# Half of a weight quarter in units 7 and 9 as separate transfers of eight partitions

## The chip, the core and the metric

The kernel runs on one core of a Trainium2 chip. The core has five engines with a queue of instructions each: TensorE (PE), VectorE (DVE), ScalarE (ACT), GpSimd (POOL) and SyncE (SP). They synchronise by semaphores. Data between the main memory and the on-chip memory of 128 partitions is moved by sixteen DMA engines, which all queues share. To tell the two kinds apart, this text always says "DMA engine" for one of those sixteen. The metric is the device time of one execution in microseconds: the median over several executions. The time before is 437.35 us, the median of three runs (436.70 to 437.56).

## The reference

The reference joins two parts. The first is causal attention over eight batches, eight heads, 576 tokens and a head size of 64, with a decay bias from a cumulated gate:

```
scores = scale * q @ k.T;   bias = -(cum[:, None] - cum[None, :])
attn   = softmax(where(causal, -1e9, scores + min(bias, 0)))
x      = attn @ v                      # heads side by side: 8 x 576 x 512
```

The second mixes the tokens in the frequency domain. It keeps 64 modes of the real Fourier transform over the tokens, and multiplies each mode by a complex 512 x 512 matrix of its own:

```
X  = rfft(x, axis=1)[:, :64]
Yr = Xr @ w_r - Xi @ w_i;   Yi = Xr @ w_i + Xi @ w_r      # per mode
u  = x + irfft(Y, n=576)
out = u + relu(u @ w_ch)
```

The weights w_r and w_i have 64 x 512 x 512 float32 values each, 134 MB together. They are most of the 163 MB that an execution reads.

## The kernel before

**Attention.** A loop over `n` in `range(N)` with N = 32 handles one batch and two heads at a time: transposes of q and k, scores, exponentials, and products with v. After each step the Fourier transform of the step's tokens is taken (`fft`, `fft_pick`). Every eight steps one group `g` of 128 of the 512 input channels is complete, and the mode products of that group can run.

**Weights.** The weights of the first three channel groups come in 24 *units* (`NUN`). A unit holds 16 modes of one group, either w_r (even units) or w_i (odd units). `unit_loads(u)` makes four lists for it, one for each quarter `h`: a quarter fills 32 partitions, from `QP * h` on, with 4 rows of 2048 values (`HU`) in each. Float32 in main memory becomes bf16 on the chip; the transfer itself converts. A quarter is one transfer of 512 KB as written, 1 MB as read, except where a first row is left out or a unit lies in two places. The weights of the fourth group come in 16 *tiles* of 64-partition transfers (`tile_loads`). Five buffers, `w_sb`, hold units and tiles in turn. Unit 7 lies in `w_sb0`, unit 9 in `w_sb2`.

**The list.** `loads_w(upto)` is what hands out the quarters in order: it takes list entries one by one, up to the number that `on_chip[n]` allows at step `n`. Entry `4 * u + h` is quarter `h` of unit `u`. `load(*lists)` merges the lists of one step (q and k, v, tails of v, weights) by their relative position, and issues them on POOL's queue, at line 315 of the kernel before. All loads of weights, q, k and v go through this one queue in this order, and an instruction that waits there holds up all behind it.

**Semaphores.** POOL's transfers use eight semaphores in turn. A transfer that takes a semaphore waits until the transfer before it on that semaphore has landed, so that at most eight are under way at a time. One transfer raises its semaphore sixteen times, once for each DMA engine, and only then has it landed.

**Consumers.** `quads` (line 605) multiplies a unit: unit 7 in step n = 14, unit 9 in step n = 17. `modes` (line 628) multiplies the tiles of the fourth group after the attention loop. The last tile's product is followed by the last transposes, the products with w_ch, and the sums and stores of the output, which have no more loads to wait for. SP's queue carries the small loads `qt<-ncum_dram`, two rows each, once per step from n = 2 on, and the stores.

Of the kernel before, what the change touches and what calls it, by code (L numbers as in the profile page):

```python
# [19 lines left out]
def kernel(  # L20
# [14 lines left out]
    DM = H * D  # L35
# [190 lines left out]
    HU = WM * DM  # L226

    def slot(i, x, n=1):

        return w_sb[i][:, x * WM : (x + n) * WM, :].rearrange("p m e -> p (m e)")  # L230
# [8 lines left out]
    def parts_of(u):  # L239

        if u == 0:
            return [(0, xg[:, : 4 * HU])]
        if u == 1:
            return [(0, ya[:, HU:]), (3, xg[:, 4 * HU : 5 * HU])]
        return [(0, slot(UNIT_AT[u], 0, 4))]

    wt = {}

    def unit_loads(u):

        g, c, ri = u // NCK, u % NCK // 2, u % 2
        src = (moe_w_r, moe_w_i)[ri][:, g * P : (g + 1) * P, :]
        slots, todo = [], []
        for j0, t in parts_of(u):
            slots += [t[:, i : i + HU].rearrange("p (q e) -> p q e", q=QD) for i in range(0, t.shape[1], HU)]
        for h in range(QD):
            todo.append([])
            for j0, t in parts_of(u):
                first = 1 if ri == 1 and c + h + j0 == 0 else 0
                j1 = j0 + t.shape[1] // HU  # L260
                todo[-1].append((
                    t[QP * h : QP * h + QP, first * HU :].rearrange("p (j x) -> p j x", x=HU),
                    src[16 * c + 4 * (j0 + first) + h : 16 * c + 4 * j1 - 3 + h : 4].rearrange(
                        "j (p q) e -> p j (q e)", q=QD
                    ),
                ))
        wt[g, c, ri] = slots
        return todo

    def tile_loads(k):  # L270

        c, ri = divmod(k, 2)
        src = (moe_w_r, moe_w_i)[ri][:, (NG - 1) * P :, :]
        i, x = TILE_AT[k]
        t = slot(i, 2 * x, 2).rearrange("p (m e) -> p m e", e=DM)
        m0 = 2 * MC * (c // 2) + 2 * (c % 2)
        todo = []
        for x0, x1 in [(0, 4)] if k < NT3 - 1 else [(0, 2), (2, 4)]:
            for h in range(2):
                first = 1 if ri == 1 and c == 0 and x0 + h == 0 else 0  # L280
                todo.append((
                    t[HP * h : HP * h + HP, 2 * (x0 + first) : 2 * x1].rearrange("p (m q) e -> p m (q e)", q=2),
                    src[m0 + 4 * (x0 + first) + h : m0 + 4 * x1 - 3 + h : 4].rearrange(
                        "m (p q) e -> p m (q e)", q=2
                    ),
                ))
        wt[NG - 1, c, ri] = [t[:, :WM], t[:, WM:]]
        n = len(todo) // 2
        return [todo[:n], todo[n:]]

    NLW = 4 * NUN + 2 * NT3
    asked, queued = [0], []

    def loads_w(upto):
        todo = []
        while asked[0] < min(upto, NLW):
            if not queued:
                t = asked[0]
                queued.extend(unit_loads(t // 4) if t < 4 * NUN else tile_loads((t - 4 * NUN) // 2))
            todo += queued.pop(0)  # L300
            asked[0] += 1
        return todo

# [45 lines left out]
    first = loads_qk(0)  # L349
    load(first[:2])  # L350
    load(loads_w(2 * W0), loads_v(0) + loads_tails(0) + first[2:] + loads_v(1))
    nc.sync.dma_start(out=Ff_sb.rearrange("p T c -> p (T c)"), in_=d_Ff)
    nc.sync.dma_start(out=G_sb[:, :S], in_=d_G)
# [265 lines left out]
    def modes(g, c, meanwhile=None):  # L619
# [16 lines left out]
        for x in range(4):  # L636
# [3 lines left out]
            for z in range(4):  # L640
                if meanwhile:
                    product(ri, z // 2, 2 * y + z % 2)
                else:
                    product(ri, y, z)
        load(loads_w(fits(NLW, 2 * NUN + 2 * c + 2)))
        yb = fpool.tile([P, DM], FP16, name="y_sb", tag="y")
        for cols in halves if c == NCK - 1 else [slice(0, DM)]:
# [65 lines left out]
    with tc.tile_pool(name="sc_psum", bufs=2, space=PSUM) as scpool, \  # L713
# [8 lines left out]
        for n in range(N):  # L722
            tails_due = loads_tails(n // B + 1)[n % B - 3 : n % B - 2] if 2 < n % B < 5 else []
            load((loads_qk(n + LA) if n % 2 else []) + (loads_vs(n) if n else loads_v(LA)) + tails_due, loads_w(on_chip[n]))
            if n == N - B:
                nc.gpsimd.dma_start(out=wch_sb, in_=moe_w_ch.rearrange("(dt p) e -> p dt e", p=P))
# [18 lines left out]
            i = first_pairs[n - N + len(first_pairs)] if n >= N - len(first_pairs) else None  # L745
# [346 lines left out]
    for step in (  # L1092
# [8 lines left out]
        i = int(step[1:].rstrip("ab"))  # L1101
# [34 lines left out]
```

## Time and profile before

| what | value |
|---|---|
| median of three runs | 437.35 us |
| the profiled execution's own time | 437.12 us |
| its span | 435.3 us |
| PE busy | 379.7 us (87%) |
| DVE, ACT, POOL busy | 254.8, 246.7, 136.5 us |
| POOL's DMA queue: packets' time as a share of 16 DMA engines' span | 99.2% |
| moved, mean rate | 93.14 MB as written, 214 GB/s |
| read from main memory | 163.29 MB |
| last weights have landed, PE starts on them | 400.41 us |

The span reaches from the first to the last instruction. Times in this text count from its start. The profiled execution lies 0.23 us below the median, and 1.8 us of its time lie outside of its span. Besides the views of engines, the trace holds a record of each DMA packet (start, duration, size, queue) and of each semaphore increment by a transfer. They don't name the DMA engine. But the sixteen increments of one transfer, put in order, show how far the sixteen DMA engines lie apart at that transfer.

### The profile page before, as it was taken

The numbers are of one execution on the slowest core, as the hardware profiler recorded it, in microseconds if no ns is written. First come the engines' busy times: TensorE is split into PE (matmuls) and PEld (weight loads), VectorE is DVE, ScalarE is ACT, GpSimd is POOL, SyncE is SP. The second block draws the span as 40 slices with busy tenths as digits, with TensorE's granted clock in tenths as the row PEclk, the third lists the DMA queues.
The fourth block names the chain that finished last, engine by engine and source line by source line (L and its number), as shares of the span: only waits on it lengthen the run. The fifth ranks groups of instructions, "written<-read, shape, count | busy, mean of one in ns | idle before, by whom it ended". The sixth has DMA issues, their size and how long they took to land. (4 is left out here: it accounts for less than half of the span.)

```text
span 435.3 us, 12579 instructions
## 1 busy us (share of the span) xinstructions
PE 379.7 (87%) x5371; PEld 219.1 (50%) x5371; DVE 254.8 (59%) x571; ACT 246.7 (57%) x552; POOL 136.5 (31%) x218
## 2 busy tenths in 40 slices
PE   1599999989999999999997888969885798796994
PEld 1256666645656655656654445535542355342441
DVE  7555666537766765677565466634644255461795
ACT  1377777726866855757774546536541255340894
POOL 6464242131432222323322222222222221310582
PEclk9999999999999999999999899999989799999998
DMA  9999999999999999999999999999999999994798
GB/s 165 209 209 209 212 209 208 213 214 212 211 209 212 209 209 213 211 212 206 213 210 213 211 212 212 212 214 213 213 210 212 211 211 211 208 219 96 224 374 307
DMA packets 47393, 93.14 MB, mean 214 GB/s; under 512 B 8254, under 2 KB 18234, under 8 KB 47338
## 3 DMA queue, kind: packets, MB, share of 16 engines
q0 software_dynamic: 40400, 81.28, 99.2%
q1 hardware_dynamic: 6938, 11.06, 7.5%
q8 instruction: 42, 0.69, 0.6%
q14 instruction: 13, 0.11, 0.1%
HBM read 163.29 MB, written 9.51 MB: 397 GB/s over the span
## 5 line engine op out<-in xcount | busy, mean ns | idle before, releaser
L513 ACT ACTIVATE p_sb<-sc_ps,cumt_sb 128x320 f16<-128x320 f32 (+1 forms) x384 | 160.6, 519 | 33.7 <-PE sc_ps L504 33.7
L504 PE MATMUL sc_ps<-qt,kt 128*64 128x256 bf16 (+3 forms) x640 | 95.6, 295 | 2.3 <-ACT kt L458 1.7
L504 PEld LDWEIGHTS <-kt 128*128 128x128 bf16 (+1 forms) x640 | 50.5, 126 | 62.9 <-issue 35.9
L315 POOL DMA_DIRECT2D w_sb<-in_moe_w_i_dram x62 | 35.2, 568 | 96.5 <-DMA w_sb<-in_moe_w_r_dram 33.9
L458 DVE COPY qt<-tr_ps 64x576 bf16<-64x576 bf16 x64 | 47.7, 746 | 20.2 <-PE tr_ps L454 19.9
L550 DVE RECIPROCAL rcp<-av_ps 128x5 f32<-128x5 f32 x64 | 12.4, 194 | 76.1 <-PE av_ps L545 75.9
L315 POOL DMA_DIRECT2D w_sb<-in_moe_w_r_dram x60 | 34.1, 570 | 71.4 <-DMA w_sb<-in_moe_w_r_dram 26.0
L493 PE MATMUL sc_ps<-negm,ident 128*128 128x512 bf16 x128 | 51.4, 401 | 0.0
L475 ACT ACTIVATE p<-sc_ps,cumt 128x64 f16<-128x64 f32 x32 | 10.0, 314 | 58.3 <-PE sc_ps L471 58.3
L545 PEld LDWEIGHTS <-p_sb 128*128 128x128 f16 x1088 | 40.4, 98 | 3.5
L454 PE MATMUL tr_ps<-ident,qk 64*64 64x64 bf16 x1152 | 31.6, 198 | 11.8 <-DVE kt L458 5.2
L454 PEld LDWEIGHTS <-qk 64*64 64x64 bf16 x1152 | 24.3, 112 | 24.1 <-DVE kt L458 8.3
L458 ACT COPY kt<-tr_ps 64x576 bf16<-64x576 bf16 x32 | 22.9, 717 | 23.5 <-DVE qt L458 23.0
L496 PE MATMUL sc_ps<-negm,ident 128*128 128x256 bf16 x128 | 36.1, 282 | 0.0
L545 PE MATMUL av_ps<-va,p_sb 128*128 128x65 f16 x768 | 34.7, 193 | 0.0
L605 PE MATMUL yp<-w_sb,xs 64*32 64x512 bf16 (+1 forms) x704 | 30.5, 403 | 4.4 <-DMA w_sb<-in_moe_w_i_dram 1.6
L551 DVE TENSOR_TENSOR x_all<-av_ps,rcp 128x320 f16<-128x320 f32 x64 | 31.5, 492 | 2.2
L617 DVE TENSOR_TENSOR y_acc<-yp,y_acc 128x512 f32<-128x512 f32 x34 | 21.9, 686 | 16.2 <-PE yp L605 16.2
L545 PE MATMUL av_ps<-vb,p_sb 128*128 128x65 f16 x320 | 25.8, 194 | 0.0
L458 DVE COPY kt<-tr_ps 64x576 bf16<-64x576 bf16 x32 | 24.4, 764 | 0.4
L315 POOL DMA_DIRECT2D vr<-in_v_dram x22 | 15.2, 692 | 28.6 <-DMA w_sb<-in_moe_w_r_dram 8.2
L605 PEld LDWEIGHTS <-xs 64*32 64x32 bf16 (+1 forms) x768 | 16.3, 139 | 14.8 <-issue 7.8
(128 smaller groups left out, 530.0 us busy)
## 6 DMA issues: line engine op xcount, KB each, us to landing
w_sb<-in_moe_w_r_dram POOLq DMA_DIRECT2D x60, 512.0 KB, 17.0
w_sb<-in_moe_w_i_dram POOLq DMA_DIRECT2D x55, 512.0 KB, 16.6
out_dram<-w_sb SPq DMA_DIRECT2D x16, 512.0 KB
qk<-in_q_dram POOLq DMA_DIRECT2D x15, 288.0 KB, 12.7
qk<-in_k_dram POOLq DMA_DIRECT2D x15, 288.0 KB, 15.3
vr<-in_v_dram POOLq DMA_DIRECT2D x14, 256.0 KB, 15.5
x_all<-in_moe_w_r_dram POOLq DMA_DIRECT2D x4, 512.0 KB, 9.7
y_acc<-in_moe_w_i_dram POOLq DMA_DIRECT2D x3, 384.0 KB, 8.0
```

The lines of the kernel that those rows point to most:

```text
L315: nc.gpsimd.dma_start(out=dst, in_=src)
L454: nc.tensor.transpose(ps[rows, r, :], src[rows, r, :], ident16[rows, rows])
L458: copy(out=to[:, :, :, half * RH : half * RH + RH], in_=ps[HP * i : HP * i + HP].rearrange("d r (h p) -> d h p r", h=2),)
L493: nc.tensor.matmul(ps[:, : 2 * W], ident16, both, start=True, stop=False, skip_group_check=True)
L496: nc.tensor.matmul(ps[:, S : S + W], ident16, negm[:, NMB + m0 : NMB + m0 + W], start=True, stop=False, skip_group_check=True,)
L504: nc.tensor.matmul(ps[rows, c0 : c0 + i1 - i0], keys, qh[:, i0:i1], start=False, stop=True, skip_group_check=True,)
L513: nc.scalar.activation(out=pt[:, o : o + n_], in_=ps[:, c0 : c0 + n_], func=ACTF.Exp, bias=cumt_sb[:, x, pidx : pidx + 1], scale=0.125,)
L545: nc.tensor.matmul(ps[:, I, :NCH], lhsT, rhs, start=(i == 0), stop=(i == len(todo) - 1), skip_group_check=True,)
L550: nc.vector.reciprocal(out=rcp, in_=ps[:, :, D])
L551: nc.vector.tensor_tensor(out=x_all[:, g, b, :, D * h : D * h + D], in0=ps[:, :, :D], in1=rcp.unsqueeze(2).to_broadcast([P, NT, D]), op=AL ...
L605: nc.tensor.matmul(ps[hp][32 * j : 32 * j + 32, :], cols[k0:k1, q_, c0 : c0 + 4 * B, 4 * c + j], wt[g, c, ri][j][k0:k1, q_, :], start=(ri ...
L617: nc.vector.tensor_tensor(out=y, in0=ps[hp], in1=y, op=ALU.add)
```

## The change

In units 7 and 9 the second quarter (`h = 1`, 32 partitions) is no longer one transfer. Its first sixteen partitions are one transfer at the same place in the list. Its other sixteen are cut into four pieces, each of eight partitions: partitions 16 to 23 whole (4 rows of 2048 values, "large"); 512 values of the last row of partitions 24 to 31 ("small"); their first three rows ("large"); and the other 1536 values of their last row ("small"). The pieces go into a list of their own, `pieces`, and `loads_w` adds one of them after each odd list entry.

```
+    ONE_HALF = (7, 9)
+    pieces = []
     wt = {}

     def unit_loads(u):
...
         wt[g, c, ri] = slots
+        if u in ONE_HALF:
+            (dst, src), = todo[1]
+            todo[1] = []
+            for i, (p0, p1, j0, j1, x0, x1) in enumerate((
+                (0, 16, 0, 4, 0, HU), (16, 24, 0, 4, 0, HU), (24, 32, 3, 4, 0, DM), (24, 32, 0, 3, 0, HU),
+                (24, 32, 3, 4, DM, HU),
+            )):
+                (pieces if i else todo[1]).append((dst[p0:p1, j0:j1, x0:x1], src[p0:p1, j0:j1, x0:x1]))
         return todo
...
             todo += queued.pop(0)
+            if asked[0] % 2:
+                todo += pieces[:1]
+                del pieces[:1]
             asked[0] += 1
```

For unit 7 the entries are 28 to 31. So the first large piece comes behind entry 29, the first small one behind 31, the second large one behind 33 and the last small one behind 35, among the quarters of unit 8. For unit 9 they stand behind entries 37, 39, 41 and 43, the last two among the quarters of unit 10. Per unit POOL issues four transfers more; the bytes are the same.

The order on POOL's queue changes in a second way, since `load` merges by relative position and the weights' lists are longer: the first quarter of unit 8 now stands ahead of the q load of its step, not behind it, and so does the third quarter of unit 9. PE's instructions keep their order; the product of each of the two units waits for the semaphores of more transfers.

## Prediction

> **What bounds the kernel now.** I read the page's DMA queues first, then PE's timeline near the end, then POOL's waits, then the packet records.
>
> ```profile
> DMA packets 47393, 93.14 MB, mean 214 GB/s; under 512 B 8254, under 2 KB 18234, under 8 KB 47338
> q0 software_dynamic: 40400, 81.28, 99.2%
> q8 instruction: 42, 0.69, 0.6%
> ```
>
> POOL's queue fills the sixteen DMA engines for the whole span by this count. PE's fetches of instructions (q8, 42 packets of 16 KB) seem nothing: 0.6%. But each such packet sits on one DMA engine for 0.95 us.
>
> ```profile
> 389.00 0.67 PE L628 MATMUL yp<-w_sb,xs 128*32 128x512 bf16 x8 [0.69 <-DMA w_sb<-in_moe_w_i_dram]
> 394.73 0.68 PE L628 MATMUL yp<-w_sb,xs 128*32 128x512 bf16 x8 [0.75 <-DMA w_sb<-in_moe_w_r_dram]
> 396.89 0.65 PE L628 MATMUL yp<-w_sb,xs 128*32 128x512 bf16 x4 [0.50 <-DMA w_sb<-in_moe_w_i_dram]
> 400.41 0.65 PE L628 MATMUL yp<-w_sb,xs 128*32 128x512 bf16 x4 [1.47 <-DMA w_sb<-in_moe_w_i_dram]
> ```
>
> PE's timeline: every product near the end waits for its weights, the last until 400.41. The 34.9 us from there to 435.3 hold no load. So the time is the landing of the last weights plus a constant.
>
> ```profile
> POOL w_sb L315 <- DMA w_sb<-in_moe_w_r_dram: 59.9, 33, 3.5
> POOL w_sb L315 <- DMA w_sb<-in_moe_w_i_dram: 32.9, 20, 2.0
> POOL qk L315 <- PE tr_ps L454: 29.9, 7, 7.5
> ```
>
> POOL's waits are mostly for transfers (eight in flight), some for a buffer that PE frees.
>
> A transfer lands when the slowest of the sixteen DMA engines has done its share. All get equal shares of every transfer now, so they should keep step. The increments show that they don't. Against the first of the sixteen, the lags are, in us:
>
> ```
> at  46 us: 0 to 1.9, evenly spread
> at 127 us: 0 .31 .44 .61 .62 .68 1.20 1.45 | 1.82 1.92 2.06 2.21 2.29 2.49 2.76 3.08
> at 379 us: 0 .45 .61 .76 .93 1.76 2.20 3.72 | 4.99 5.40 5.44 5.76 6.36 6.55 6.62 6.89
> last one : 0 .07 .17 .56 .82 .83 1.75 2.74  | 4.44 4.49 4.79 5.18 5.37 5.56 5.90 6.89
> ```
>
> Eight are late and eight early, with a gap of 1.3 us between the groups at 379 us. Each 16 KB fetch in the stretch from 290 to 330 us pushes one of the late eight on by about 0.9 us, none of the early; eight times five fetches make the distance (42 x 0.95 / 8 = 5.0 us). So the last landing, 400.37, is a late one's; the last early one is done at 393.48 + 2.74 = 396.22.
>
> **The change part by part.** *Shares.* A packet of 2048 values (8 KB read, 4 KB written) takes 0.322 us and the next starts 0.019 us before its end: 0.303 us each. Sixteen partitions spread over sixteen DMA engines are 4 such packets on each. As pieces of eight partitions they can occupy eight DMA engines at a time; if consecutive pieces alternate between two halves, the half that gets the large ones does 4 + 3 = 7 packets and the other 0.25 + 0.75 = 1. That is +0.91 and -0.91 us per unit, +1.82 and -1.82 for both units.
>
> *Which half.* No row of before has a transfer of eight partitions. The nearest are the thirty two-row loads `qt<-ncum_dram` of SP: two packets of 0.064 us. At the one of 300 us two lags move by 0.06 (1.74 to 1.80, 3.40 to 3.46), both in the early eight, and the fourteen others stay; earlier loads agree. A short transfer thus begins among the early eight. I take it that POOL's begin there too: the first piece, a large one, on the early half, the second on the late half. The other sign is the far bound.
>
> [...]
>
> *More transfers.* Four more per unit are eight more, each with an increment on every DMA engine. Landings of transfers of sixteen packets of 0.153 us lie 2.486 us apart between 345 and 379 us, so that one transfer costs 2.486 - 2.448 = 0.04 us beside its packets: +0.3 us on all sixteen (0, if a piece burdens only its own half).
>
> *POOL's queue.* Eight more issues at 0.56 us (rows of L315) are 4.5 us on an engine that is 31% busy. Between two issues at 114 to 120 us it waits 1.7 us for landings: this hides them. Ahead of the q load at 111.04 and the one at 127.29, which wait 7.47 and 3.52 us for PE, one more weight quarter is now issued; q and k of that step come one quarter, 2.5 us, later. The k load of 112.18 lands at 124.3 and its transposes run at 131.2, so this is free. SP's queue isn't passed.
>
> *Eight in flight.* Small pieces take semaphores too. The leanest window, behind unit 8 (two v tails, a small and a large piece, 16 partitions, three whole quarters), holds 0.42 + 0.42 + 1.2 + 1.2 + 2.43 + 2.43 + 1.83 = 9.9 us on the early half. The early ones' lead there is 3.1 us and an issue takes some 3 us until its first packets (the one of 374.59 until about 377.5): 3.8 us are left, nothing runs dry.
>
> *Late pieces.* Unit 7's last piece stands behind the transfer that lands at 132.2 us and PE reads unit 7 at 138.81; unit 9's stands behind the one of 159.0 and is read at 164.79. Neither wait binds, by 5 to 6 us; if that cover were gone, PE's excess would be paid in full only where PE later lacks slack, since weights bound the end.
>
> *Sum.* Late half: 400.37 - 1.82 + 0.3 = 398.85. Early half: 396.22 + 1.82 + 0.3 = 398.34. The late half still ends last, 1.5 us earlier. What is late next is the early half, half a microsecond behind. The execution's 437.12 becomes 435.6; with its 0.23 us to the median, 435.9 us. Bounds from the increments' price: 435.5 to 435.9.
>
> **The rivals.** *The wrong half.* The large pieces go to the late half: 400.37 + 1.82 + 0.3 = 402.5, the time 437.35 + 2.1 = 439.5. For it: no row shows where POOL's queue starts a short transfer, and the early eight need not be the same eight as a piece's. Against it: the two-row loads. It decides as soon as the large pieces' eight hold the latest DMA engine.
>
> *Crowded partitions.* Eight DMA engines write eight neighbouring partitions. The nearest rows are SP's stores `yv<-y_sb` and `yv<-v_sb` into sixteen partitions: the first two after 400 us moved 262 KB in 1.74 us (151 GB/s, 9.4 per partition), the third 131 KB in 1.38 us (5.9 per partition). The weights' stream writes 4096 B in 0.303 us, 13.5 GB/s per partition. At those rates a large packet would take 0.44 to 0.69 us, fourteen of them 1.9 to 5.4 us more. The early half would end at 400.2 to 403.7 and the time be 437.2 to 440.7. It decides against the change above 0.14 us more per packet (398.34 + 2.03 = 400.37). Against it: the same stores peak at 32 packets in 0.1 us, 20 GB/s per partition, and DMA engines that lie up to 1.5 us apart don't write together throughout. I take no stretch and keep it as a rival.
>
> [...]
>
> *No shift.* If a piece of eight partitions is cut finer and spread over all sixteen, only the increments are left: +0.3 us, 437.7. Against it: nothing but the equal shares of now, which are of sixteen partitions and more.
>
> **How the numbers follow.** About 0.2%, 0.87 us, is what a measurement of this kernel can tell from no change. The forecast has 0.54 (faster 0.52, as the gain may be eaten below 0.87 us; same 0.02). The wrong half has 0.20, slower. Crowding has 0.17: same 0.06, slower 0.11. No shift has 0.06, same. A late piece that PE does wait for has 0.03, slower. So faster 0.52, same 0.14, slower 0.34. The predicted time is the forecast's, 435.9; its own range is 435.2 to 436.4 (a further fetch of 0.95 us on the last DMA engine or one less, and the spread of the runs). The range for 8 in 10 reaches from there over crowding to the wrong half: 435.2 to 439.6; what it leaves out is crowding at its worst and luck below.
>
> **What would show it.** Right: at 379 us the late eight lie 3.6 us nearer to the early ones, the greatest lag is about 3.7 us, the last weights land near 398.9 and the tail stays 34.9 us. Wrong half: the gap grows to some 5 us and PE's last wait ends near 402.5. Crowding: packets of 2048 values longer than 0.322 us around 110 to 165 us. No shift: the lags as before. A late piece: a wait of PE at its product of unit 7 or 9. The prediction is wrong if the eight that the pieces reach aren't the early eight, whatever else holds.

## The result, and the profile after

The changed kernel takes 439.90 us, the median of six runs (438.38 to 441.22); the kernel before, beside it on the same chip, 437.39 us. The ratio is 1.0057, with a 95% interval of 1.0044 to 1.0071: slower by some 2.5 us, where a gain of 1.5 us was forecast. The profiled execution of the changed kernel took 441.22 us, 1.3 us above its median, with a span of 439.4 us. Where the time went is read from its span, what it is worth from the medians.

The DMA queues' part of the page of the changed kernel (queue: packets, MB, share of sixteen engines' span):

```profile
DMA packets 47682, 93.14 MB, mean 212 GB/s; under 512 B 8527, under 2 KB 18523, under 8 KB 47627
q0 software_dynamic: 40688, 81.28, 99.7%
q8 instruction: 42, 0.69, 0.6%
```

The bytes are the same, PE's fetches are the same 42, and POOL's queue still fills the sixteen DMA engines for the whole span. They only took longer. PE's timeline near the end (start, duration, line, operation, idle time before it and what ended it), to be set against the four lines of before in the prediction:

```profile
392.23 0.67 PE L641 MATMUL yp<-w_sb,xs 128*32 128x512 bf16 x8 [0.72 <-DMA w_sb<-in_moe_w_i_dram]
397.82 0.66 PE L641 MATMUL yp<-w_sb,xs 128*32 128x512 bf16 x8 [0.59 <-DMA w_sb<-in_moe_w_r_dram]
400.13 0.65 PE L641 MATMUL yp<-w_sb,xs 128*32 128x512 bf16 x4 [0.66 <-DMA w_sb<-in_moe_w_i_dram]
403.37 0.65 PE L641 MATMUL yp<-w_sb,xs 128*32 128x512 bf16 x4 [1.19 <-DMA w_sb<-in_moe_w_i_dram]
```

The last landing still decides: it comes at 403.33 us instead of 400.37. The rest of the 4.1 us of the span lies behind it: from PE's last start on weights to the end it is 36.0 us instead of 34.9, at a granted clock of 0.90 instead of 0.95 over this part.

Where the 3 us arose shows in the table of stretches (from and to in us, length, busy time and instructions of PE, PEld, DVE, ACT and POOL, PE's clock, DMA share, GB/s). Before:

```profile
90.00:130.00 40.00, 38.70 (x690) 23.70 (x683) 25.54 (x58) 24.04 (x57) 11.38 (x19) 1.00 1.12 211
130.00:170.00 40.00, 38.82 (x646) 23.74 (x646) 24.52 (x58) 26.45 (x64) 11.37 (x20) 1.00 1.11 210
170.00:400.00 230.00, 200.69 (x2737) 114.65 (x2735) 124.57 (x264) 114.98 (x253) 57.24 (x97) 0.96 1.09 208
```

After:

```profile
90.00:130.00 40.00, 38.70 (x687) 23.63 (x687) 25.49 (x58) 23.79 (x56) 12.65 (x22) 1.00 1.16 202
130.00:170.00 40.00, 37.23 (x620) 22.60 (x616) 23.69 (x56) 26.30 (x62) 14.25 (x25) 0.99 1.14 202
170.00:400.00 230.00, 202.33 (x2756) 116.13 (x2756) 125.65 (x265) 115.75 (x254) 58.23 (x98) 0.95 1.10 211
```

In the two stretches that hold the pieces of units 7 and 9 the rate falls by 9 and 8 GB/s: 40 us x 17 GB/s are 0.68 MB less, which at 0.211 MB per us is 3.2 us. At the same time the DMA share *rises*, from 1.12 to 1.16: more time in packets, fewer bytes. So it isn't a queue that ran empty. The DMA queues in one stretch of 8 us, 109 to 117 us, make it plainer. Before:

```profile
DMA packets 936, 1.69 MB, mean 211 GB/s; under 512 B 61, under 2 KB 575, under 8 KB 935
q0 software_dynamic: 931, 1.67, 112.7%
```

After:

```profile
DMA packets 855, 1.33 MB, mean 166 GB/s; under 512 B 95, under 2 KB 597, under 8 KB 854
q0 software_dynamic: 850, 1.31, 134.5%
```

A fifth of the bytes is missing in these 8 us, and the packets' summed time is longer. By the packet records a packet of 2048 values takes 0.322 to 0.324 us nearly everywhere, in both kernels. From 109.5 to 114.5 us of the changed kernel its median is 0.494 us, nine tenths are below 0.638, the longest takes 0.792; from 134.5 to 139.5 us the median is 0.444, the longest 0.791. These are the places of the transfer of sixteen partitions and of the first large piece behind it, once for each unit. What these packets take above 0.323 us adds up to 48.6 us from 105 to 150 us (2.6 before), that is 46/16 = 2.9 us for each of the sixteen DMA engines, the size of the delay.

The lags, from the order of the increments as in the prediction, at the transfer eleventh from the end:

```
before, 371.7 to 378.6 us : 0 .45 .61 .76 .93 1.76 2.20 3.72 | 4.99 5.40 5.44 5.76 6.36 6.55 6.62 6.89   mean landing 375.40
after,  375.2 to 381.8 us : 0 .37 .99 1.19 1.67 3.20 3.38 4.32 4.51 5.49 5.67 5.75 6.02 6.08 6.21 6.62     mean landing 379.06
```

The greatest lag is 6.6 us where 3.7 was forecast: the late ones came no nearer. The mean landing is 3.7 us later: all sixteen lost time, not one half.

### The profile page after: what moved, and what is told of

Read it like the earlier page. It is cut to its first block, busy times and chain, and to the rows that moved or that the text cites. A ratio compares the mean times of both kernels' runs of the same rounds, so it can differ in the third digit from the quotient of the medians.

```text
span 439.4 us, 12588 instructions
## 1 busy us (share of the span) xinstructions
PE 383.9 (87%) x5371; PEld 221.3 (50%) x5371; DVE 254.7 (58%) x571; ACT 247.3 (56%) x552; POOL 141.1 (32%) x226
## 5 line engine op out<-in xcount | busy, mean ns | idle before, releaser
L517 PE MATMUL sc_ps<-qt,kt 128*64 128x256 bf16 (+3 forms) x640 | 97.0, 298 | 1.5 <-ACT kt L471 0.8
L328 POOL DMA_DIRECT2D w_sb<-in_moe_w_i_dram x70 | 39.7, 568 | 103.5 <-DMA w_sb<-in_moe_w_r_dram 37.9
L471 DVE COPY qt<-tr_ps 64x576 bf16<-64x576 bf16 x64 | 47.7, 746 | 21.9 <-PE tr_ps L467 21.6
L328 POOL DMA_DIRECT2D qk<-in_q_dram x17 | 10.3, 606 | 40.4 <-PE tr_ps L467 29.1
```

Of the source, the lines that this page charges most:

```text
L328: nc.gpsimd.dma_start(out=dst, in_=src)
L471: copy(out=to[:, :, :, half * RH : half * RH + RH], in_=ps[HP * i : HP * i + HP].rearrange("d r (h p) -> d h p r", h=2),)
L517: nc.tensor.matmul(ps[rows, c0 : c0 + i1 - i0], keys, qh[:, i0:i1], start=False, stop=True, skip_group_check=True,)
```

## Experiments

Two things had to be explained: 2.5 us more, and a gain of 1.5 us that didn't come. Theory 1 (crowding): transfers into few neighbouring partitions are slower in themselves. Rival (wrong half): the large pieces push the late DMA engines. For the missing gain: the pieces' halves aren't the early and the late eight, or they don't alternate as taken.

In the edits, a row of the list is (first partition, end, step, first row, end row, first value, end value) of the quarter; and the lines with + stand for the whole list of the changed kernel, where nothing else is said.

**Partitions apart.**

```
-                (0, 16, 0, 4, 0, HU), (16, 24, 0, 4, 0, HU), (24, 32, 3, 4, 0, DM), (24, 32, 0, 3, 0, HU),
-                (24, 32, 3, 4, DM, HU),
+                (0, 32, 2, 0, 4, 0, HU),
+                (1, 32, 4, 0, 4, 0, HU),
+                (3, 32, 4, 3, 4, 0, DM),
+                (3, 32, 4, 0, 3, 0, HU),
+                (3, 32, 4, 3, 4, DM, HU),
```

> As the changed kernel, but each transfer takes partitions that lie apart: the sixteen are every second of the 32, the two groups of eight every fourth. Same bytes, packets and places in the list. Crowded partitions: packets of 2048 values go back to 0.322 us throughout, the 2.5 us of slowdown are gone, and what is left is the shift between the halves: 435.9 us if the large pieces go to the early half, 439.5 if to the late half. Rival, pieces cost by their number (increments and small packets): stays near 439.9 with no long packets.

Measured: 436.78 us (12 runs) beside 437.04 of before, ratio 0.9999 (0.9983 to 1.0015). The same sizes, the same number of transfers in the same places, and the loss is gone. Neither of the two shifts that were to be left, to 435.9 or to 439.5 us, came either. The stretch from 109 to 117 us and the two long stretches of this kernel:

```profile
DMA packets 968, 1.70 MB, mean 212 GB/s; under 512 B 118, under 2 KB 621, under 8 KB 967
q0 software_dynamic: 963, 1.68, 113.0%
...
90.00:130.00 40.00, 38.70 (x673) 23.55 (x673) 24.83 (x57) 23.61 (x56) 13.28 (x23) 0.96 1.11 211
130.00:170.00 40.00, 38.81 (x645) 23.54 (x643) 23.93 (x58) 26.50 (x63) 13.73 (x25) 1.00 1.13 209
```

211 and 209 GB/s, as before. The packets above 0.323 us make 4.5 us from 105 to 150 us instead of 48.6. So the loss hangs on which partitions a transfer writes, not on its size, its half or its place in the list.

**The same, small pieces first.** The edit is to the kernel with partitions apart; the order of the pieces becomes small, large, small, large.

```
-                (1, 32, 4, 0, 4, 0, HU),
                 (3, 32, 4, 3, 4, 0, DM),
-                (3, 32, 4, 0, 3, 0, HU),
+                (1, 32, 4, 0, 4, 0, HU),
                 (3, 32, 4, 3, 4, DM, HU),
+                (3, 32, 4, 0, 3, 0, HU),
```

> As the run with partitions apart, but small pieces first: small, large, small, large. If pieces alternate between halves, this is its mirror: 439.5 us where that one has 435.9, and the other way round; the gap between the late and the early eight moves by 3.6 us in opposite directions in the two. If pieces don't alternate, or spread over all sixteen DMA engines, both have the same time, near 437.7.

Measured: 436.89 us (12 runs), ratio 0.9999 (0.9985 to 1.0013). If one order helped the late half, the other had to hurt it. Neither does anything: the greatest lag near 378 us is 6.5 us in the one and 6.8 in the other.

**Two transfers of sixteen neighbours, no pieces.**

```
+                (0, 16, 1, 0, 4, 0, HU),
+                (16, 32, 1, 0, 4, 0, HU),
```

Both stand at the quarter's own place in the list.

> The quarter of units 7 and 9 goes as two transfers of sixteen neighbouring partitions at its old place; no pieces, no shift. Crowding by sixteen neighbouring partitions: long packets around both units, some 2 us slower (439.4). Crowding only by eight: packets of 0.322 us, 437.4 to 437.6.

Measured: 440.25 us (4 runs), ratio 1.0084 (1.0056 to 1.0111). No transfer of eight partitions is left here, and the sixteen increments are all that two transfers more bring (3216 packets of four bytes instead of 3184), so by these counts none leaves DMA engines out, and the loss is as large as with the pieces. This kernel from 109 to 117 us, and its last wait for weights:

```profile
DMA packets 872, 1.48 MB, mean 185 GB/s; under 512 B 66, under 2 KB 580, under 8 KB 870
q0 software_dynamic: 866, 1.45, 124.1%
```

```profile
402.28 0.65 PE L641 MATMUL yp<-w_sb,xs 128*32 128x512 bf16 x4 [1.44 <-DMA w_sb<-in_moe_w_i_dram]
```

The lags keep the two groups of before (eight up to 3.07, eight from 4.73 to 5.88 us), 1.7 us later in the mean. That is the wrong half's end as a reason for the loss. The longer packets account for (29.4 - 2.6) / 16 = 1.7 us here, and the profiled execution, the fastest of the four, is 2.1 us above that of before; why the median is another microsecond higher is not settled.

**Two transfers of sixteen, partitions apart.**

```
+                (0, 32, 2, 0, 4, 0, HU),
+                (1, 32, 2, 0, 4, 0, HU),
```

> The quarter of units 7 and 9 as two transfers of sixteen partitions that lie apart (every second row), no pieces of eight. If neighbours are what crowds: packets stay at 0.322 us, only two more transfers' increments are left (0.08 us), 437.1 to 437.6. If a transfer of sixteen partitions is dear however its rows lie: near the 440.25 us of the two transfers of sixteen neighbouring partitions.

Measured: 437.17 us (10 runs), ratio 1.0005 (0.9991 to 1.0019). Against the run above only the step between the partitions differs. Neighbouring is what costs here (440.25 against 437.17 us); a transfer of sixteen partitions in itself costs nothing that can be measured.

**The sixteen neighbours alone.** The transfer of partitions 0 to 15 is kept, the eights behind it lie in every second partition of 16 to 31.

```
+                (0, 16, 1, 0, 4, 0, HU),
+                (16, 32, 2, 0, 4, 0, HU),
+                (17, 32, 2, 3, 4, 0, DM),
+                (17, 32, 2, 0, 3, 0, HU),
+                (17, 32, 2, 3, 4, DM, HU),
```

> The changed kernel's transfer of sixteen neighbouring partitions (rows 0 to 15) is kept, but the two eights behind it are interleaved (rows 16, 18, ... and 17, 19, ...), large and small as there. If the transfer of sixteen neighbours carries the crowding: two of them here against four in the run of two sixteens each (440.25 us) make half of its 2.9 us: 438.5 to 439.0. If the pieces of eight neighbours carry it: 437.0 to 437.5. If eight in every second row of sixteen crowd as well: 439.5 to 440, as the changed kernel.

Measured: 438.72 us (6 runs) beside 437.13, ratio 1.0026 (1.0011 to 1.0042): within what was expected if the sixteen neighbours carry it. From 109 to 117 us:

```profile
DMA packets 907, 1.49 MB, mean 186 GB/s; under 512 B 103, under 2 KB 611, under 8 KB 906
q0 software_dynamic: 902, 1.47, 120.5%
```

The longer packets are 21.6 us from 105 to 150 us, (21.6 - 2.6) / 16 = 1.2 us for each DMA engine. So of the changed kernel's loss about 1.1 us (0.0026 of the time; 0.5 to 1.8 us by the interval) belong to the two transfers of sixteen neighbours. The rest, some 1.4 us (0.0057 - 0.0026), goes away when the eights lie in every second partition: by this difference it belongs to the pieces of eight neighbours.

**Even pieces.** Partitions apart, the second sixteen as two pieces of eight with four rows each.

```
+                (0, 32, 2, 0, 4, 0, HU),
+                (1, 32, 4, 0, 4, 0, HU),
+                (3, 32, 4, 0, 4, 0, HU),
```

> Partitions apart, and two pieces of eight partitions with four whole rows each instead of large and small: if pieces alternate, both halves get four packets, no shift. The lags at the end are those of the kernel before within 0.3 us, and the time is 437.4 plus 0.2 for four more transfers: 437.6. A cost by the number of pieces would show as more than that.

Measured: 437.11 us (10 runs), ratio 1.0000 (0.9983 to 1.0017). Four transfers more cost nothing that can be measured. The lags near the end differ from those of before by up to 0.8 us, where at most 0.3 was expected.

What became of the shares is read from the landings. If the earliest DMA engine has no share in a piece, the earliest increment moves by the transfer's own burden alone, some 0.17 us (the least in the table below); if it has a share of four or three packets of 0.303 us, by 1.2 or 0.9 us. For the latest likewise. How far the earliest and the latest increment moved at the large pieces (us, earliest / latest):

```
                 unit 7: first large   second large     unit 9: first large   second large
changed kernel     .33 / 1.17           1.38 / .34        .17 / 1.19           1.26 / .52
apart              .42 / .62             .93 / .20        .17 / 1.26            .99 / .37
small first        .41 / 1.76            .90 / .95        .17 / .86             .90 / .31
even pieces        .17 / .93            1.18 / .80        .17 / 1.03           1.19 / .23
```

In all eight units the second large piece moves the earliest increment by 0.90 us or more, and the first one by 0.42 at most. At unit 9, where the first large piece moves it by no more than 0.17 us in any of the four kernels, the reading is plain: the first large piece leaves the earliest DMA engine alone and the second one loads it. So a large piece does go to eight DMA engines, four packets each (it has 32, and 4 x 0.303 = 1.2 us is what an even piece moves the increment by, 1.18 and 1.19), but *the two large pieces of a unit go to different halves*, although a small piece stands between them in three of these kernels. The halves get 4 and 3 of the large packets, not 7 and 0, and what was to be shifted cancels within the unit.

**Eight units, to see it often.** Both edits are to the kernel with partitions apart. First with all four pieces directly one behind another in one list entry, then with one at every second entry.

```
-    ONE_HALF = (7, 9)
+    ONE_HALF = range(5, 21, 2)
...
-                (pieces if i else todo[1]).append(...)
+                (pieces if i > 9 else todo[1]).append(...)
```

The second of the two has only the first of these edits.

> Partitions apart, but in eight units (every odd one from 5 to 19) and the four pieces directly one behind another in one list entry: large (4 rows), small (a quarter row), large (3 rows), small (three quarters of a row). Theory A, each piece goes to the other half than the piece before: one half gets 7 packets and the other 1 in every unit, 8 x 0.91 = 7.3 us more on one half and 7.3 less on the other, so that the greatest distance in step grows from 6.9 to over 10 us and the time by 3 us (all heavy ones early before) to 8 us (late ones among them). Theory B, the half is tied to the rows (or only the large pieces turn it): the two large pieces of a unit go to different halves and cancel, 437.0 to 438.5 (32 more increments, 0.04 us each, at most), distances as before.

> As e6, the same pieces in the same eight units, but one at every second list entry as in the changed kernel. If what lies between two pieces turns the half as well, the distances differ from those of e6; if not, they are as in e6, whichever theory holds there. Time as e6, plus PE's waits for late pieces if any bind.

Measured: 439.73 us (3 runs), ratio 1.0050 (1.0033 to 1.0067), directly one behind another; 439.45 us (6 runs), ratio 1.0041 (1.0023 to 1.0059), one at every second entry. The distances don't grow to 10 us: they are 3.9 and 4.6 us near the end. The landings at the pieces speak against theory A in both. In the second kernel the reading is without exception: at the first large piece of all eight units the earliest increment moves by 0.17 to 0.27 us and the latest by 0.89 to 1.39; at the second large piece the earliest by 0.94 to 1.38 and the latest by 0.20 to 0.36. What lies between two pieces has no part in it: where they stand directly one behind another, the second large piece moves the earliest increment further than the first, too, in all eight units.

The times were expected below 438.5 by theory B, and are a microsecond above. 32 transfers more are not free: the mean landing near 378 us is 4.8 and 4.2 us later, of which longer packets make 2.2 and 2.4 us. And fewer than sixteen packets were under way for 6.0 and 3.9 us (summed over the missing ones), where in the kernel before it is 0.0 from 80 to 370 us. Some DMA engines ran dry here, and the distances came out smaller (3.9 and 4.6 us instead of 6.89). That the one made the other is the author's reading; by it these distances say little on shares, and the landings do. Why packets got longer here, with partitions apart, no run shows.

**What turns the half.** As the first of these two (eight units, directly one behind another), with 3 and 1 whole rows for each eight partitions, and with 2 and 2.

```
+                (1, 32, 4, 0, 3, 0, HU),
+                (1, 32, 4, 3, 4, 0, HU),
+                (3, 32, 4, 0, 3, 0, HU),
+                (3, 32, 4, 3, 4, 0, HU),
```

> As the one before, but the pieces of the first eight rows are 3 and 1 whole rows, and of the second eight 3 and 1. Theory A (each piece turns): 6 packets against 2 in every unit, 8 x 0.61 = 4.8 us more on one half: 438 to 445 us and distances that show it. Theory B in the form that rows decide: 4 against 4, 437.0 to 438.5. Theory B in the form that only pieces of whole rows turn it: as A.

```
+                (1, 32, 4, 0, 2, 0, HU),
+                (1, 32, 4, 2, 4, 0, HU),
+                (3, 32, 4, 0, 2, 0, HU),
+                (3, 32, 4, 2, 4, 0, HU),
```

> As e7, but every piece has 2 whole rows: two pieces of the first eight partitions (every fourth row from 1), then two of the second eight (every fourth row from 3), directly one behind another. If the rows decide the half: the first two pieces fall on the same eight DMA engines, whose landings go 1.2 us apart from the others' after the second piece, and the last two level them again. If each such piece goes to the other half than the piece before: 0.6 us apart after the first piece, level after the second, and so on. Time 437.5 to 439.5 by both (32 more transfers).

Measured: 439.05 us (4 runs), ratio 1.0040 (1.0021 to 1.0059), and 438.24 us (8 runs), ratio 1.0039 (1.0018 to 1.0060). The first time falls in the range of theory A, but the distances (3.7 us) don't, and the queue ran dry as above (3.1 and 5.5 us): the time tells nothing apart here. The landings do. With 2 and 2 the earliest increment moves by turns less and more, in six of the eight units, though clearly, by 0.16 us and more from piece to piece, only in four (in one of them .20, .52, .19, .57): each piece of two rows goes to the other half than the piece before it. The first two have the same partitions, so it isn't the rows that decide. With 3 and 1 the two pieces of three rows go to different halves again (plainly in five of the eight units, where the earliest moves by 0.17 or 0.18 and then by 0.6 to 1.0 us), with a piece of one whole row between them.

Together: in these runs pieces of two and more rows took the halves by turns, and a piece of one row didn't count in the turns. Why that is so no run shows, nor which DMA engines a piece of one row uses: it moves the earliest and the latest increment too little to tell (the first small pieces of the changed kernel by 0.30 and 0.26 us in unit 7, 0.17 and 0.22 in unit 9).

**Pieces that all count.** If this is right, large and small do come to lie on different halves when the small ones have four rows too. Partitions apart, units 7 and 9, one piece at every second entry:

```
+                (1, 32, 4, 0, 4, 0, DM // 4),
+                (3, 32, 4, 0, 4, 0, HU),
+                (1, 32, 4, 0, 4, DM // 4, DM // 2),
+                (1, 32, 4, 0, 4, DM // 2, HU),
```

> Partitions apart, units 7 and 9, one piece at every second list entry, but all four pieces have four rows each: small (128 values of each row of the first eight partitions), large (all of the second eight), small (128 more values), large (the other 1792). If pieces of more than one row go to the two halves by turns, small ones included, and the first of a unit to the half that holds the latest DMA engine, the half of the earliest takes about 1.0 us more per unit and the other 1.0 us less: the large pieces push the earliest landing by 1.1 to 1.4 us and leave the latest, the greatest distance at 379 us falls from 6.9 to about 3, and the time to 435.5 to 436.3 if the latest DMA engines all lie in the light half; 437.0 to 439.5 if some of the late ones lie in the heavy half. If the halves can't be steered by the order: one large piece pushes the latest, the other the earliest, and the time is that of before, 437.0 to 437.8.

The same pieces, large first:

```
+                (3, 32, 4, 0, 4, 0, HU),
+                (1, 32, 4, 0, 4, 0, DM // 4),
+                (1, 32, 4, 0, 4, DM // 2, HU),
+                (1, 32, 4, 0, 4, DM // 4, DM // 2),
```

> The same pieces, large first: large, small, large, small. If the turns hold, both large pieces of a unit push the latest landing and leave the earliest, the latest get 2.0 us more, and the time is 438.8 to 440. If the order steers nothing: 437.0 to 437.8, as its mirror image.

Measured: small first 443.77 us (5 runs) beside 437.77, ratio 1.0142 (1.0120 to 1.0165); large first 438.54 us (12 runs), ratio 1.0024 (1.0013 to 1.0036). With large first the turns hold: all four large pieces move the latest increment (by 1.29, 1.08, 1.75 and 1.05 us) and leave the earliest (by 0.17 to 0.27), and the greatest lag becomes 8.99 instead of 6.89 us, 2.1 more, where 2.0 were expected. The time rose by 0.8 to 1.1 us, less than expected. It can't be put down to the shift alone: packets above 0.323 us sum to 50.5 us in this kernel, 28.6 before, which is 1.4 us for each DMA engine. And the mirror image didn't do as expected. With small first the large pieces were to move the earliest increment by 1.1 to 1.4 us and leave the latest; they moved the earliest by 0.60, 0.29, 0.21 and 0.30 us and the latest by 1.83, 1.37, 1.94 and 1.65. So with either order all four large pieces burden late DMA engines. The lags at the transfer eleventh from the end:

```
large first: 0 .49 3.43 3.66 4.38 4.81 5.24 5.44 5.49 5.53 5.64 6.06 6.14 | 8.12 8.71 8.99
small first: 0 .10 .48 1.07 1.74 1.82 1.84 2.11 | 3.77 3.84 6.41 | 8.70 8.79 9.04 9.37 9.75
```

With large first three DMA engines stand out as the latest, with small first five. If the heavy halves of the two kernels are each other's complement, three of the late eight lie in one half of the pieces and five in the other. That fits the three and the five, and large pieces that burden late ones in either order, but it is worked out and not shown: no record names the DMA engine. It would mean that a piece's half always holds late ones, and neither order can bring the last landing forward.

Small first is slower by far more than its shares give. Its packets above 0.323 us sum to 92.0 us over the whole trace, 28.6 before, which is 4.0 us for each DMA engine; 39.3 of the 92.0 lie between 145 and 165 us. The stretch from 130 to 170 us of small first, and then of large first:

```profile
130.00:170.00 40.00, 37.90 (x624) 23.02 (x622) 24.17 (x58) 26.30 (x63) 12.74 (x22) 1.00 1.15 198
```

```profile
130.00:170.00 40.00, 37.87 (x634) 22.96 (x632) 24.18 (x57) 25.99 (x62) 13.98 (x24) 0.99 1.12 208
```

198 against 208 GB/s, with the same pieces in another order and no neighbours among them. What makes packets longer there stays open. No kernel tried is faster than the one before by more than the noise.

## Why the prediction was wrong, step by step

Two things went wrong. The gain of 1.5 us didn't come, by two steps that failed ("Shares" and "Which half"), and 2.5 us were lost that went away with partitions apart ("Crowded partitions"): 435.9 + 1.5 + 2.5 = 439.9, the median measured.

*"I take no stretch" (Crowded partitions).* This step failed, and it cost the most. The rival was named with its sign, a chance of 0.17 and 437.2 to 440.7 us, and it is what happened: the packets were longer around 110 and 137 us, as the list of signs had it. Two things were wrong in how it was weighed. It was priced for the large pieces alone, on the half that they fall on. But the transfer of sixteen neighbours, for which the sum had no extra cost at all, was crowded as well; it alone makes about 1.1 us, and with two transfers of sixteen neighbours and no pieces both groups of lags moved together, 1.7 us in the mean. And it was dismissed by one row, stores whose peak was 20 GB/s per partition, and by lags of 1.5 us that were to keep the DMA engines from writing together. The packets measured, 0.444 and 0.494 us in the median instead of 0.322, lie within the bounds that the prediction had worked out from the rates of those stores (0.44 to 0.69); the longest, 0.79, lie above them.

The runs show the crowding as a difference: 440.25 us with two transfers of sixteen neighbours, 437.17 us with the same number of partitions apart. Why neighbours make packets longer no run shows.

*"If consecutive pieces alternate between two halves" (Shares).* Failed for these pieces. Large pieces do burden eight DMA engines with four and three packets, as taken. But the small pieces have one row, and the next large piece goes to the other half all the same, so that the halves get 4 and 3. No run shows the +1.82 and -1.82 us of the sum: that small and large pieces alternate was the author's assumption. In their place the first large piece moved the latest increment by 1.17 and 1.19 us in the changed kernel, and the second the earliest by 1.38 and 1.26. With pieces that all count, large first, the greatest lag grew as worked out (2.1 us).

*"A short transfer thus begins among the early eight" (Which half).* Failed. The evidence was from two-row loads of SP's queue; POOL's first large piece left the earliest DMA engine alone in both units (its increment moved by 0.33 and 0.17 us, the latest by 1.17 and 1.19). The last sentence of the prediction named this as what would make it wrong. By the two runs with pieces that all count, the late eight seem to lie in both halves.

*More transfers.* Held in size: four more cost nothing that can be measured (ratio 1.0000), eight more neither (0.9999), with +0.3 us forecast. A DMA engine without a share in a piece pays 0.17 us for it, though, not 0.04, and 32 more were 1.7 to 2.2 us slower, parts of which are longer packets and a queue that ran dry.

*Eight in flight.* Held for two units: in the changed kernel, too, sixteen packets and more were under way from 80 to 370 us throughout. With eight units and four pieces in each the queue ran dry (3.1 to 6.0 us, summed over the missing packets).

*Late pieces.* Held: in the changed kernel PE doesn't wait for weights at the products of units 7 and 9 (from 139.37 and 165.25 us).

*POOL's queue.* The step costed the later q and k loads at nothing. One wait that wasn't there before came, on another load of k, further on:

```profile
170.56 0.69 PE L467 MATMUL tr_ps<-ident,qk 64*64 64x64 bf16 x17 [2.14 <-DMA qk<-in_k_dram]
```

PE waits 2.1 us for k at 170 us. It has time to make this up, since the weights decide the end; with partitions apart there is no such wait from 130 to 172 us. So it goes with the crowding.

*What decides the end.* Held in the kernel before and the changed one, where PE waits 1.47 and 1.19 us for the last landing. The tail was taken as a constant 34.9 us; it was 36.0 in this profiled execution. But a second limit lies close behind the last landing, and the sum had no term for it. With partitions apart PE waits for SP's store `yv<-v_sb`, and from there on the trace shows no gap up to the last product on weights:

```profile
394.76 0.61 PE L923 MATMUL z_ps<-yv,G_sb 96*128 96x512 f16 x2 [1.88 <-DMA yv<-v_sb]
399.35 0.65 PE L644 MATMUL yp<-w_sb,xs 128*32 128x512 bf16 x4
```

The last weights landed at 399.30 us there. Had they landed earlier still, as the forecast wanted (398.85), PE, busy until then, could have gained little by it in this kernel.

The rival "wrong half" gave 439.5 us, close to the measured time, by a cause that the runs rule out: without any transfer of eight partitions the time is 440.25 us, and the changed kernel's greatest lag is 6.6 us, not more than before. A time that fits is no proof of its mechanism.

## What to carry to other kernels

When a transfer is cut by partitions, cut it so that each part still spreads over the partitions that the whole reached (every second or fourth one), not into blocks of neighbours: here that was worth 2.5 us with the same bytes, sizes and order. It isn't enough by itself: in the kernels with pieces in eight units (but for the one with 2 and 2 rows) and in the two with pieces that all count, packets got longer with partitions apart too (47.7 to 92.0 us above 0.323 in sum, 28.6 before), for reasons that are open. A DMA share that rose while GB/s fell (1.12 to 1.16, 211 to 202 GB/s from 90 to 130 us) came with longer packets in the changed kernel (0.494 us in the median from 109.5 to 114.5 us, instead of 0.322 to 0.324), and there it was what they wrote to that counted: with partitions apart 1.11 and 211 GB/s. Before work is shifted from late to early DMA engines, show which of them a short transfer reaches, on the queue that issues it and at the sizes that it will have; here pieces with several rows per partition took two halves by turns, and pieces with one row didn't count in the turns.

## What had not been expected of the hardware

- With transfers into sixteen neighbouring partitions, and eights of neighbours behind them, packets of 2048 values took 0.494 us in the median (109.5 to 114.5 us, changed kernel) instead of 0.322 to 0.324, up to 0.79; with the sixteen in every second partition and the eights in every fourth, the median stayed at 0.324.
- Of transfers of eight partitions on POOL's queue, those with two and more rows per partition took two halves of the DMA engines by turns (with four and three rows in all eight units of one run: the earliest increment moved by 0.17 to 0.27 us at the first large piece, by 0.94 to 1.38 at the second; with two rows in six units of eight, clearly in four); one with one row, between them, didn't count in the turns.
- Such a transfer cost a DMA engine that has no share in it 0.17 us at the least (0.17 to 0.27 in that run), and brought four-byte packets beside the sixteen increments: by the counts of the runs, one for each packet of its data (partitions times rows). The changed kernel has 3456 of them against 3184, 128 increments and 144 = 2 x 8 x 9 more (its pieces have 4, 1, 3 and 1 rows in each of two units); with the even pieces there are 3376, 64 increments and 128 = 2 x 8 x 8. Transfers of sixteen partitions brought none (3216 with two more: 32 increments).
- Two kernels with the same four pieces in another order differ by 5.2 us (443.77 and 438.54). Longer packets make (92.0 - 50.5) / 16 = 2.6 us of it for each DMA engine, most of them at 145 to 165 us; their cause and the rest are open.
